# One core, FNet mixing with a gated FFN: the hidden transform's matrix sums made partly by adding DMAs, one input chunk brought back early into another buffer, two silus moved

## The chip, the cores and the metric

The kernel runs on one core of a Trainium2 chip. The time is device microseconds of one execution, smaller is better. The kernel before took 766.7 us (median of three runs, 765.25 to 767.39).

## The reference

```python
x = A_x                                   # 1 x 2048 x 448
xn = layernorm(x)
a, b = xn @ dft_hid_re.T, xn @ dft_hid_im.T     # 448 x 448 each
s = dft_seq_re @ a - dft_seq_im @ b             # 2048 x 2048 each
g = silu((gelu(xn @ w_gate) * (xn @ w_up)) @ w_down)   # 448 -> 1792 -> 448
out = x + s * g
```

All of it is float32. The kernel reaches that precision with float32r matmuls: a matrix is split into a high half (a copy rounded to float32r, made by ACT) and a low half (what is left, a subtraction on DVE), and a product is high·high + high·low + low·high.

## The kernel before

**Data.** The 2048 rows of x are 16 tiles of 128, in four chunks of four tiles. After the norm and the transposes, chunk c lies with its high and low half in the buffer `a_x[c]` (128 x 4096; `xt` in the profile).

**First stage, the FFN.** It runs from the start to about 397 us. The first two of the 14 feature blocks f are done plainly; the other twelve are done twice, for chunk pair p = 0 and p = 1, by a Strassen scheme: 24 calls of `strassen(f, p, ...)`, one after the other, a call taking PE 13.73 us in the steady state. In a call PE makes the products x1, x2, x3, x6, x4, then the second parts of x1, x6 and x4 (in this order, with the down products `po` of the group before between them). DVE adds the products up (L503, L511, L519, L539, L555 and others), ACT makes the gelu (L526, L558) and the high halves. Each product has a PSUM bank; the next call's x1 and x4 use the banks that this call's gelu (L526) and last addition (L555) read.

The lists `prep` and `dn` hold what else a call has to issue, at fixed places: `prep[0]` behind u (L503) and ahead of c21 (L511), `prep[1]` behind L519, `prep[2]` behind the gelu of x1. `prep` carries the weights of the next call: the low halves of the plain blocks and, on POOL, `sums_s` (five additions and subtractions, L337 to L343, of the raw weights); then ACT's high halves of these sums (`high`, L356, L357); then DVE's low halves (`low`, L360, L361) and SP's load of the weights for the call behind. Every third call adds two big DMAs (L957): the first terms of the sequence matrices' sums are copied from DRAM to DRAM, 896 KB each, and two calls later POOL issues two DMAs that add the second terms (L959; the queue `adds` is emptied inside `sums_s`, behind its first instruction).

**Matrices of the hidden transform.** The hidden transform uses the same scheme and needs sums of the blocks of its own matrices `et`. They are made in the calls of p = 1, appended to `prep` by `e_steps(f)`: in f = 5 to 9 five full-width subtractions, two full-width additions and a half-height subtraction of 448 columns (`e_sum`, L1054), two low halves of 896 columns (`es_low`, L1062) and, for the second set, high and low halves in f = 9 (L1067, L1068, L1071, L1075). The second set is stored to `eq` at f = 10 and loaded back at f = 13 (`eq_load`).

**Middle stage, the hidden transform.** Its order is the table `HID`, read word by word: `0.mm` are the 22 matmuls of row tile 0 (plain, tiles 0 to 7, chunks 0 and 1), `0.ev`, `0.sm`, `0.ca`, `0.lo` its way from PSUM (ACT), its sums (DVE, L1364 to L1367), high half (ACT, L1386) and low half (DVE, L1389). `P0` to `P3` are the paired tiles 8+kk and 12+kk. `s.3` and `s.all` are the last eight down products of the FFN (PE, L439, `po`), each followed by one DVE addition (L452); they use three PSUM banks in turn. Chunk 1 was written to DRAM (`sp`) in the first pass, since its buffer `a_x[1]` then held sums of chunk 2 and 3 until `P3`; `x.0` to `x.3` bring it back into `a_x[1]`, two DMAs each. Tile 4 (`4.mm`, L1266) is the first that reads it.

**Last stage, the sequence transform.** From about 477 us on, 8 output pairs j of 16 units: 14 units of seven products (`seven`, L1524 and L1527, 14 matmuls, some 2.18 us of PE each) and two plain ones (`py`, L1550). Each unit's matrix piece is loaded, summed (`sum_c`, L1434, L1435), and split by ACT (`high_c`, L1442) and DVE (`low_c`, L1446) three units ahead. All 14 transformed tiles (`TS`) stay in SBUF but four, in two pairs (`KX`), which are stored (`td`, POOL, L1391) and swapped in and out. At the end `gather` puts the seven products together on DVE, `g_` is the silu of the last two rows' gates, and L1645 to L1656 make and store the last two output tiles.

Instructions are issued in the order in which the code records them, on each engine's own queue.

Of the kernel before, what the change touches and what calls it, by code (L numbers as in the profile page):

```python
# [8 lines left out]
F32 = mybir.dt.float32  # L9
# [4 lines left out]
P = 128  # L14
# [28 lines left out]
KR = (8, 12, 9, 13, 10, 11, 4, 5, 6, 7)  # L43
KX = ((0, 1), (2, 3))
# [8 lines left out]
0.mm l.0 l.1 s.3 0.ev 0.sm 0.ca s.all 0.lo g.st 1.mm 1.ev 1.sm  # L53
# [3 lines left out]
P1.x4b P1.ae P1.se 3.mm P1.ce P1.lc 3.ev P1.le 3.sm  # L57
P2.x1 P2.m 3.ca P2.x2 P2.u P2.x3 P2.c21 P2.x4 P2.be 3.lo P2.x1b P2.ac P2.x6 P2.bc P2.sc
P2.x4b P2.ae
P3.x1 P3.m P2.ce P2.cc P3.x2 x.3 P3.u P3.x3 x.2 P3.c21 P2.le P3.x4 x.0 P3.be P2.lc P3.x1b P3.ac  # L60
P3.x6 x.1 P3.bc P3.sc P3.cc P3.x4b P3.ae c.l0
4.mm P3.ce P3.lc P3.le c.l1 c.l2 t.0 t.1 4.ev 4.sm 4.ca c.s0 c.s1
# [13 lines left out]
def fnet_geglu(ctx: ExitStack, tc: tile.TileContext, xw, ca, ct, cp, et, wss, wd, out):  # L76
# [495 lines left out]
    with tc.manual_schedule():  # L572
# [461 lines left out]
        eq = dram.tile([P, 6 * D], F32, name="eq")  # L1034
# [5 lines left out]
        def e_begin():  # L1040
            ew[0] = sb.tile([P, 4096], F32, name="ew", tag="u0")
            for b in range(2):
                nc.sync.dma_start(e_part(2 * b, 2), et[b].rearrange("p r d -> p (r d)"))

        def e_next():
# [6 lines left out]
        def e_sum(to, a, b, minus=True, n=P):  # L1052
            to, a, b = [e_part(i)[:n] for i in (to, a, b)]
            return lambda: (nc.vector.tensor_sub if minus else nc.vector.tensor_add)(to, a, b)  # L1054
# [698 lines left out]
```

## Time and profile before

| | us |
|---|---|
| median of three runs | 766.7 |
| the profiled execution | 767.89 |
| its span, first to last instruction | 766.1 |
| PE busy | 757.9 |
| DVE busy | 658.0 |
| ACT busy | 355.0 |
| POOL busy | 119.7 |

The granted PE clock is 1.00 over the whole span. Rows of a timeline read: start and length in us, engine, line, operation, output<-inputs, shapes, how many, and in brackets how long the engine was idle before and who ended that. In a table of waits a row reads: who waited <- for whom: us in total, times, longest. In the list of DMA issues the last number is the time from issue to landing. PE's matmuls overlap, so two rows' distance, not one row's length, is what a matmul costs.

### The profile page before, as it was taken

What the parts mean: (1) busy time and instruction counts of PE and PEld (TensorE: products, weight loads), DVE (VectorE), ACT (ScalarE), POOL (GpSimd) and SP (SyncE); (2) the same over time, 40 slices, a digit from 0 to 9 for tenths busy, and PEclk for the clock granted to TensorE, in tenths of its full rate; (3) what the DMA queues carried; (4) which work ended last, traced back from release to release, by engine and by line L of the source; (5) the groups of instructions that cost most, each with busy time, mean ns of one, the idle gap of its engine ahead of it and who ended that gap; (6) DMA issues with size and microseconds to landing.
All of it is one profiled execution on the core that took longest, in us unless ns stands there. A gap on an engine that the chain in (4) does not pass through costs nothing.

```text
span 766.1 us, 11581 instructions
## 1 busy us (share of the span) xinstructions
PE 757.9 (99%) x4033; PEld 681.8 (89%) x4033; DVE 658.0 (86%) x1121; ACT 355.0 (46%) x511; POOL 119.7 (16%) x160
## 2 busy tenths in 40 slices
PE   9999999999999999999999999999999999999997
PEld 8988888888888888888889988999999999999997
DVE  7987789899999889999876988788888797979796
ACT  6866443444434335343432546445445354444451
POOL 1002332412424224224200000000000000000000
PEclk9999999999999999999999999999999999999999
DMA  8077584949567784739544357779796969788793
GB/s 299 15 223 233 119 249 133 239 150 245 202 153 288 180 307 132 228 99 311 136 169 180 169 181 274 246 248 324 225 352 206 342 208 314 226 300 288 235 321 142
DMA packets 83643, 170.31 MB, mean 222 GB/s; under 512 B 8320, under 2 KB 63488, under 8 KB 81792
## 3 DMA queue, kind: packets, MB, share of 16 engines
q1 hardware_dynamic: 78256, 143.05, 53.8%
q0 software_dynamic: 5184, 26.41, 16.0%
q8 instruction: 31, 0.51, 0.3%
q14 instruction: 28, 0.23, 0.1%
q10 hardware_dynamic: 144, 0.11, 0.0%
HBM read 146.01 MB, written 52.63 MB: 259 GB/s over the span
## 4 chain that ended last, share of the span: by engine, by line
PE 86%; DVE 8%; DMA 2%; issue 2%; ACT 1%; SPq 0%; DVEq 0%
PE p L1524 21%; PE x L465 19%; PE po L439 15%; PE p L1527 10%; PE ab L1266 4%; PE py L1550 4%; PE hx L1305 4%; PE x L477 3%; PE gu L388 3%; PE gu L621 2%; PE pt L223 1%; DMA xt<-sp 1%; DVE tmp L562 1%; DVE ew L1054 1%; DVE gacc L452 1%
## 5 line engine op out<-in xcount | busy, mean ns | idle before, releaser
L439 PE MATMUL po<-wd,hs 128*128 128x448 f32 x672 | 146.1, 366 | 0.0
L439 PEld LDWEIGHTS po<-wd,hs 128*128 128x128 f32 x672 | 125.7, 188 | 12.5 <-DVE gacc L452 0.3
L465 PE MATMUL x<-xt,w 128*128 128x512 f32 x432 | 112.6, 391 | 0.5 <-DVE tmp L519 0.5
L465 PEld LDWEIGHTS x<-xt,w 128*128 128x128 f32 x432 | 80.8, 188 | 17.2 <-DVE tmp L519 1.4
L465 PE MATMUL x<-t,w 128*128 128x512 f32 x276 | 80.3, 390 | 0.7 <-DVE tmp L555 0.7
L1442 ACT ACTIVATE w<-raw 128x896 fp32r<-128x896 f32 (+1 forms) x58 | 52.7, 910 | 55.9 <-PE p L1524 21.2
L452 DVE TENSOR_TENSOR gacc<-gacc,po 128x448 f32<-128x448 f32 x96 | 58.7, 613 | 6.6 <-PE po L439 6.5
L542 ACT ACTIVATE hs<-tmp 128x512 fp32r<-128x512 f32 x24 | 15.2, 633 | 102.4 <-DVE tmp L540 102.4
L465 PEld LDWEIGHTS x<-t,w 128*128 128x128 f32 x276 | 51.7, 188 | 11.0 <-DVE tmp L555 1.1
L1576 POOL DMA_DIRECT2D cc<-xw x14 | 12.3, 879 | 280.8 <-DVE raw L1434 111.7
L1524 PE MATMUL p<-xt,xt 128*128 128x448 f32 x168 | 54.4, 374 | 0.0
L1524 PE MATMUL p<-ts_g,w 128*128 128x448 f32 x168 | 54.3, 374 | 0.0
L337 POOL TENSOR_TENSOR raw<-raw 128x256 f32<-128x256 f32 x23 | 20.0, 868 | 215.4 <-DMA raw<-wss 188.2
L1442 ACT ACTIVATE w<-f 128x896 fp32r<-128x896 f32 (+1 forms) x37 | 33.0, 892 | 40.5 <-PE p L1527 15.5
L1527 PE MATMUL p<-xt,xt 128*128 128x224 f32 x168 | 44.4, 264 | 0.0
L1527 PE MATMUL p<-ts_g,w 128*128 128x224 f32 x168 | 44.4, 264 | 0.0
L1446 DVE TENSOR_TENSOR w<-raw,w 128x896 fp32r<-128x896 f32 (+1 forms) x39 | 40.7, 1045 | 3.5 <-ACT w L1442 2.7
L1524 PE MATMUL p<-xt,w 128*128 128x448 f32 x112 | 36.4, 374 | 0.0
L1524 PE MATMUL p<-hs,w 128*128 128x448 f32 x112 | 36.0, 374 | 0.0
L1266 PE MATMUL ab<-w,xt 128*128 128x448 f32 x128 | 33.8, 369 | 1.5 <-DMA xt<-sp 1.5
L356 ACT ACTIVATE w<-raw 128x768 fp32r<-128x768 f32 x24 | 20.2, 843 | 31.8 <-POOL raw L343 31.6
L1524 PEld LDWEIGHTS p<-ts_g,w 128*128 128x128 f32 x168 | 31.5, 188 | 2.4
(304 smaller groups left out, 1865.0 us busy)
## 6 DMA issues: line engine op xcount, KB each, us to landing
sums<-ca SPq DMA_DIRECT2D x16, 896.0 KB, 8.7
sums<-ca POOLq DMA_DIRECT2D x16, 896.0 KB, 9.9
raw<-ct SPq DMA_DIRECT2D x69, 192.0 KB, 4.2
raw<-wss SPq DMA_DIRECT2D x24, 512.0 KB, 3.6
xt<-td SPq DMA_DIRECT2D x24, 448.0 KB, 5.5
ts_g<-td SPq DMA_DIRECT2D x24, 448.0 KB, 6.3
raw<-sums SPq DMA_DIRECT2D x69, 128.0 KB, 4.0
f<-ct SPq DMA_DIRECT2D x43, 192.0 KB, 3.6
```

Source lines behind the costliest of these rows:

```text
L388: nc.tensor.matmul(ps[:, cols], a, xt[:, k, cols], start=n == 0, stop=n == len(mm) - 1)
L439: nc.tensor.matmul(po[:, :D], hs[:, a, kk * P : (kk + 1) * P], wdn[:, b, i], start=n == 0, stop=n == 5,)
L452: nc.vector.tensor_add(ga, ga, po[:, :D])
L465: nc.tensor.matmul(ps, a[i], b[j], start=first and n == 0, stop=n == 2, skip_group_check=True)
L477: nc.tensor.matmul(ps, a[0], x_, start=False, stop=True, skip_group_check=True)
L1266: nc.tensor.matmul(ps[r], x_, e, start=start_, stop=stop_, skip_group_check=True)
L1305: nc.tensor.matmul(ps[i], a[:, sl], b, start=first and n == 0, stop=n == len(mm) - 1, skip_group_check=True,)
L1442: nc.scalar.activation(c_hl[m][0], raw_at(m)[:, :n], AF.Copy)
L1446: nc.vector.tensor_sub(l, raw_at(m)[:, : h.shape[-1]], h)
L1524: nc.tensor.matmul(ps[q][:, :D], h, v, start=u % UN == 0, stop=False, skip_group_check=True)
L1527: nc.tensor.matmul(ps[q][:, :HD], l, v[:, :HD], start=False, stop=u % UN == NS - 1, skip_group_check=True,)
L1550: nc.tensor.matmul(p[:, e], w, v[:, e], start=n == 0, stop=n == 11)
```

## The change

1. **Matrix sums.** Two sums of the hidden matrices are no longer made on DVE. `e_first()`, called at p = 1, f = 2, has SP copy two pieces of `et` from DRAM to DRAM (`e1`, 128 x 448 each) and appends three adding DMAs to `adds`, which POOL issues inside `sums_s` of that call. The first set's remaining sums stay in f = 5 and 6; its high half is recorded one place later (`prep[2]`), its low halves go to f = 7 and f = 9 behind L519; the second set's sums go from f = 8 to f = 11. The second set is stored raw, and its high and low halves (`eq_high`, `eq_low`) are made at the start of the middle stage: `q.h` behind `l.0`, `q.l` behind `s.3`.
2. **Chunk 1.** It comes back in one DMA (`x.1`) into chunk 0's buffer `a_x[0]`, recorded behind `3.mm`, the last tile of chunk 0. Tile 0's transform is loaded into `a_x[1]` (`t.0`) behind `P3.x6`, which moves ahead of `P3.x1b`. `4.mm` takes the usual order.
3. **Another tile is kept.** The pair (2, 3) that is swapped becomes (2, 8); tile 3 stays, in `a_h[1]`, and tile 8 is stored.
4. **Silus.** The two silus of the last pair stood ahead of the first copy of the last `gather`; now one stands a unit earlier and the other behind that copy; the loads of their inputs are one unit earlier.

```diff
-KR = (8, 12, 9, 13, 10, 11, 4, 5, 6, 7)
-KX = ((0, 1), (2, 3))
+KR = (12, 9, 13, 10, 3, 11, 4, 5, 6, 7)
+KX = ((0, 1), (2, 8))
 HID = """
-0.mm l.0 l.1 s.3 0.ev 0.sm 0.ca s.all 0.lo g.st 1.mm 1.ev 1.sm
+0.mm l.0 q.h l.1 s.3 q.l 0.ev 0.sm 0.ca s.all 0.lo g.st 1.mm 1.ev 1.sm
...
-P1.x4b P1.ae P1.se 3.mm P1.ce P1.lc 3.ev P1.le 3.sm
+P1.x4b P1.ae P1.se 3.mm x.1 P1.ce P1.lc 3.ev P1.le 3.sm
...
-P3.x1 P3.m P2.ce P2.cc P3.x2 x.3 P3.u P3.x3 x.2 P3.c21 P2.le P3.x4 x.0 P3.be P2.lc P3.x1b P3.ac
-P3.x6 x.1 P3.bc P3.sc P3.cc P3.x4b P3.ae c.l0
-4.mm P3.ce P3.lc P3.le c.l1 c.l2 t.0 t.1 4.ev 4.sm 4.ca c.s0 c.s1
+P3.x1 P3.m P2.ce P2.cc P3.x2 P3.u P3.x3 P3.c21 P2.le P3.x4 P3.be P3.x6 t.0 P2.lc P3.bc
+P3.x1b P3.ac P3.sc P3.cc P3.x4b P3.ae c.l0
+4.mm P3.ce P3.lc P3.le c.l1 c.l2 t.1 4.ev 4.sm 4.ca c.s0 c.s1
...
+        e1 = [dram.tile([P, D], F32, name=f"e1{i}") for i in range(2)]
+
+        def e_first():
+            for i in range(2):
+                nc.sync.dma_start(e1[i], et[3 * i, :, 1])
+            adds.append(lambda: nc.gpsimd.dma_start(e1[0], et[1, :, 1], accum_op=ALU.add))
             for r in (slice(0, 64), slice(64, P)):
-                nc.sync.dma_start(e_part(4)[r], et[2, :64, 1])
-            nc.sync.dma_start(e_part(7), et[2, :, 1])
...
+                adds.append(
+                    lambda r=r: nc.gpsimd.dma_start(e1[1][r], et[2, :64, 1], accum_op=ALU.add)
+                )
...
         def eq_high():
-            nc.scalar.activation(e_part(0, 2).bitcast(FR), e_part(7, 2), AF.Copy)
-            nc.scalar.activation(e_part(2, 2).bitcast(FR), e_part(5, 2), AF.Copy)
+            raw = a_r[:, 4 * D : 6 * D]
+            nc.scalar.activation(a_ws[:, 4480:][:, : 2 * D], eq_raw(), AF.Copy)
+            for i, k in enumerate((5, 4)):
+                nc.scalar.activation(eq_at(k), raw[:, i * D : (i + 1) * D], AF.Copy)
...
         def eq_low():
-            nc.vector.tensor_sub(e_part(7, 2).bitcast(FR), e_part(7, 2), e_part(0, 2))
-
-        def eq_stack():
-            h = e_part(2, 2)[64:]
-            nc.vector.tensor_sub(h.bitcast(FR), e_part(5, 2)[64:], h)
+            h = a_ws[:, 4480:][:, : 2 * D]
+            nc.vector.tensor_sub(a_ws[:, 4480 + 2 * D :][:, : 2 * D], eq_raw(), h)
+            raw = a_r[:, 4 * D : 6 * D]
+            for i, k in enumerate((5, 4)):
+                h = eq_at(k)[64:]
+                nc.vector.tensor_sub(h, raw[64:, i * D : (i + 1) * D], h.bitcast(F32))
...
-            if f == 5:
-                return [e_sum(4, 1, 3, False), e_sum(6, 0, 1), e_sum(5, 4, 0)]
-            if f == 6:
-                return [e_sum(7, 2, 5), es_high, es_low(0)]
-            if f == 7:
-                return [es_low(1), e_next]
-            if f == 8:
-                return [e_sum(5, 3, 4, False), then(e_sum(6, 2, 3), e_sum(7, 5, 2, n=64)), e_sum(8, 0, 7)]
-            if f == 9:
-                return [eq_high, eq_low, eq_stack]
-            return []
+            return {
+                5: [e_sum(6, 0, 1), e_sum(5, 4, 0)],
+                6: [e_sum(7, 2, 5), nop, es_high],
+                7: [nop, es_low(0)],
+                9: [nop, es_low(1), e_next],
+                11: [e_sum(6, 2, 3), e_sum(7, 5, 2, n=64), then(e_sum(8, 0, 7), eq_store)],
+            }.get(f, [])
...
                 dn[3] = then(send2, *t1_steps[7][:2])
+                e_first()
...
-            3: lambda: a_x[0],
+            3: lambda: a_h[1],
...
-            7: lambda: a_x[1],
+            7: lambda: a_x[0],
...
-        def load_1(k):
-
-            for i in range(2):
-                v, w = [u[:, 2048 * i + 512 * k :][:, :512] for u in (a_x[1].bitcast(F32), sp)]
-                nc.sync.dma_start(v, w)
+        def load_1():
+            nc.sync.dma_start(a_x[0].bitcast(F32), sp)
...
-        orders = {4: (3, 2, 0, 1), 7: (2, 0, 1, 3)}
+        orders = {7: (2, 0, 1, 3)}
...
-        GX_AT, GX_END = (NS, 0), NS - LAST - 3
+        GX_AT, GX_END = (NS, 0), NS - LAST - 4
...
                 prep_c(m + 3)
                 prep_c(m + 4)
-                for v, w in zip(g_, gx):
-                    nc.scalar.activation(v, w, AF.Silu)
 
                 c12_6, c11_2, c21_7, c12_5, c22_5, c12_3, c21_4 = gather(ps)
+                nc.scalar.activation(g_[0], gx[0], AF.Silu)
...
+                if end and u == NS - LAST - 1:
+                    nc.scalar.activation(g_[1], gx[1], AF.Silu)
```

Two places show how instructions move. Lines are those of the kernel that a listing belongs to; `[waits ...]` names the semaphores that an instruction waits for, DMAHW those of SP's DMAs, DMASW those of POOL's.

POOL in the call p = 1, f = 2, `sums_s` of the next weights, before:

```order
L337 TENSOR_TENSOR raw<-raw 128x2x128 [waits DMAHW4_49,DMAHW3_49,DVE_49]
L340 TENSOR_TENSOR raw<-raw 128x2x128
L341 TENSOR_TENSOR raw<-raw 128x128 [waits Pool_49]
L342 TENSOR_TENSOR raw<-raw 64x128
L343 TENSOR_TENSOR raw<-raw 128x256 [waits Pool_49]
```

and now (`e_813`, `e_814` are the two `e1`):

```order
L337 TENSOR_TENSOR raw<-raw 128x2x128 [waits DMAHW4_49,DMAHW3_49,DVE_49]
L1057 DMA e_813<-et 128x448 [waits DMAHW0_49,DMASW2_49]
L1060 DMA e_814<-et 64x448 [waits DMAHW1_49,DMASW3_49]
L1060 DMA e_814<-et 64x448 [waits DMASW4_49]
L340 TENSOR_TENSOR raw<-raw 128x2x128
L341 TENSOR_TENSOR raw<-raw 128x128 [waits Pool_49]
L342 TENSOR_TENSOR raw<-raw 64x128
L343 TENSOR_TENSOR raw<-raw 128x256 [waits Pool_49]
```

Between the first addition and the other four stand three DMA issues now, and the first two of them wait for SP's two copies of `et` into `e1`.

DVE at the start of the middle stage, the additions of the last down products (L452) and tile 0's sums (L1364 to L1367), before:

```order
L452 TENSOR_TENSOR gacc_2200<-gacc_2200,po_2_2_3447 128x448
L1364 TENSOR_TENSOR raw<-raw 128x224
L1365 TENSOR_TENSOR raw<-raw 128x224
L1366 TENSOR_TENSOR raw<-raw 128x224
L1367 TENSOR_TENSOR raw<-raw 128x224
L452 TENSOR_TENSOR gacc_2200<-gacc_2200,po_2_3_3462 128x448
```

and now:

```order
L452 TENSOR_TENSOR gacc_2207<-gacc_2207,po_2_2_3448 128x448
L1087 TENSOR_TENSOR w<-w 128x896
L1091 TENSOR_TENSOR w_3185<-raw,w_3185 64x448
L1091 TENSOR_TENSOR w<-raw,w 64x448
L1376 TENSOR_TENSOR raw<-raw 128x224
L1377 TENSOR_TENSOR raw<-raw 128x224
L1378 TENSOR_TENSOR raw<-raw 128x224
L1379 TENSOR_TENSOR raw<-raw 128x224
L452 TENSOR_TENSOR gacc_2207<-gacc_2207,po_2_3_3466 128x448
```

Three subtractions (`q.l`) stand between the third and the fourth addition of a down product, ahead of tile 0's sums.

More of the change, by code (lines that the diff above doesn't have):

```diff
@@ L1033, in fnet_geglu @@
         gv = gs.rearrange("p (k d) -> p k d", k=NK)
-        eq = dram.tile([P, 6 * D], F32, name="eq")
+        eq = dram.tile([P, 4 * D], F32, name="eq")
         ew, es, w2 = [None], [None], [None]
@@ L1329, in high_e @@
                     return
-                h, l = [rest(v) for v in ((new["tmp"], a_x[0]), (new["u1"], new["u0"]))[ke - 14]]
+                h, l = [rest(v) for v in ((new["tmp"], new["u1"]), (new["u0"], a_x[1]))[ke - 14]]
                 v = fs[ke][:, : 2 * D]
@@ L1412, in slot_at @@
                 lambda: (unit_at(2), unit_at(3)),
-                lambda: (unit_at(4), rest(a_x[1])),
+                lambda: (unit_at(4), rest(a_x[0])),
             )[m % 4]()
```

27 lines of the change are left out of this document (15 added, 12 removed).

## The prediction

> **What bounds the kernel now.** I read the page first, then PE's own waits, then PE's timeline call by call, and last the rows of the engines that PE waits for.
>
> ```profile
> PE 757.9 (99%) x4033; PEld 681.8 (89%) x4033; DVE 658.0 (86%) x1121; ACT 355.0 (46%) x511; POOL 119.7 (16%) x160
> ```
>
> PE is the bound, and the change leaves its matmuls as they are: the same number, another order. So only the few microseconds in which PE does not run can be won, and every new wait of PE is a loss. PE's waits in the middle of the kernel are three:
>
> ```profile
> PE ab L1266 <- DMA xt<-sp: 1.5, 1, 1.5
> ...
> PE x L465 <- DVE tmp L555: 0.7, 1, 0.7
> PE x L465 <- DVE tmp L519: 0.5, 1, 0.5
> ```
>
> A wait of PE costs a little more than its row, because the pipeline fills again. What they cost is read from the starts of the calls (x1 of f = 5, 6 and 11 in the second pass):
>
> ```profile
> 271.40 0.86 PE L465 MATMUL x<-xt,w 128*128 128x512 f32 x3
> ...
> 285.14 0.86 PE L465 MATMUL x<-xt,w 128*128 128x512 f32 x3
> ...
> 355.85 0.86 PE L465 MATMUL x<-xt,w 128*128 128x512 f32 x3
> ```
>
> f = 5 takes 285.14 - 271.40 = 13.74 us without a wait; six calls take 84.45, that is 2.05 us more than six times 13.73 or so (82.4). That is all there is in the first stage of this pass.
>
> **The change part by part.** The sum is made against the profiled execution, 767.89 us (its span 766.1), which is 1.2 us above the median 766.7; I apply it to the median.
>
> *A, the sums on DVE: -2.05.* DVE does its share of a call in order, so what the matrix sums add makes all behind them late. The first operation on x2 (L503) shows by how much:
>
> ```profile
> L1054 DVE TENSOR_TENSOR ew<-ew 128x448 f32<-128x448 f32 x7 | 5.4, 772 | 0.0
> ...
> 274.18 0.69 DVE L503 TENSOR_TENSOR tmp<-tmp,x 128x512 f32<-128x512 f32 x1 [1.51 <-PE x L465]
> ...
> 304.00 0.68 DVE L503 TENSOR_TENSOR tmp<-tmp,x 128x512 f32<-128x512 f32 x1
> ...
> 306.93 1.08 DVE L1062 TENSOR_TENSOR es<-ew,es 128x896 fp32r<-128x896 f32 x1
> ...
> 347.48 0.67 DVE L503 TENSOR_TENSOR tmp<-tmp,x 128x512 f32<-128x512 f32 x1
> ...
> 358.80 0.68 DVE L503 TENSOR_TENSOR tmp<-tmp,x 128x512 f32<-128x512 f32 x1
> ```
>
> At 274.18 DVE still waits for PE. Two calls on, PE's product is ready at 274.18 + 27.47 = 301.65, but DVE comes at 304.00, 2.35 late, and with L1062's 1.08 ahead of c21 it is 3.4 late at L519: PE stops for the 0.5. In the call from 347.48 to 358.80 DVE has no matrix work and needs 11.32 us, 2.4 less than PE. Up to that first stop the change takes out one full-width addition (0.77 by its group's row) and one low half (1.08), and moves the other low half behind L519, so DVE is some 2.9 less late there, far from a stop. Up to the second (L555, f = 9 to 10) f = 8's four operations and one of f = 9's two go as well. Three of these come back in f = 11: 3 x 0.77 = 2.3 in an odd call, which has another low half of its own, of 1.08 like L1062's; 11.32 + 1.08 + 2.3 = 14.7, one microsecond over PE's 13.73, well below the 3.4 at which PE stopped. I take all 2.05. The bounds are 1.0 (one stop stays) and 2.05.
>
> *B, chunk 1: -2.2, of which about 0.9 comes back, so -1.3.*
>
> ```profile
> 436.29 4.46 PE ab L1266 x22
> ...
> 456.40 2.37 PE L1266 MATMUL ab<-w,xt 128*128 128x448 f32 x10
> 460.30 1.70 PE L1266 MATMUL ab<-w,xt 128*128 128x448 f32 x6 [1.54 <-DMA xt<-sp]
> ...
> 463.09 0.37 PE L1266 MATMUL ab<-w,xt 128*128 128x448 f32 x1
> ```
>
> A tile needs 4.46; tile 4 took 463.09 - 456.40 = 6.69, so 2.23 are lost to the load. The new load waits for tile 3, whose 4.46 end at 440.75, and has 15 us until tile 4 at 456.40; it is 2 MB in one DMA, and a pair of 896 KB copies with a load behind it takes 9.1 us (in D). It is in time. But PE then reaches the last stage 2.23 earlier, and DVE does not:
>
> ```profile
> 463.25 0.39 DVE L1364 TENSOR_TENSOR f<-f 128x224 f32<-128x224 f32 x1 [0.63 <-ACT f L1374]
> ...
> 484.69 1.08 DVE L1446 TENSOR_TENSOR xt<-f,xt 128x896 fp32r<-128x896 f32 x1
> ...
> 485.50 0.38 PE L1524 MATMUL p<-w,xt 128*128 128x448 f32 x1
> 485.82 0.37 PE L1527 MATMUL p<-w,xt 128*128 128x224 f32 x1
> ```
>
> The first product of the fifth unit uses the high half at 485.50, and its second, with the low half, follows 0.32 later instead of the usual 0.21: DVE's 484.69 + 1.08 = 485.77 was only just in time. DVE is busy nearly throughout from tile 4's sums to there. It can move up by the 0.63 at its first row and by the short waits for ACT behind it, which I put at 0.7 together; 1.3 of 2.23. PE then waits some 0.9 at this unit. Bounds for B: 0 (DVE does not move up) and -2.23.
>
> *C, the silus: -0.35.*
>
> ```profile
> 751.62 1.04 ACT L1628 ACTIVATE raw<-ts_g 128x448 f32<-128x448 f32 x2 [0.23 <-DVE w L1446]
> ...
> 753.13 0.62 DVE L1559 TENSOR_TENSOR cc<-cc,p 128x448 f32<-128x448 f32 x1 [0.94 <-ACT cc L1557]
> ...
> 762.46 0.38 DVE L1650 TENSOR_TENSOR f<-raw,py 128x224 f32<-128x224 f32 x1
> ```
>
> From 753.13 on DVE runs to the end without a pause. The copy L1557 stood behind the two silus (751.62 + 1.04 = 752.66), and its product was done when the first of them began or shortly after: some 0.6 to be had. The last L1650 can come no earlier than PE's last matmul, around 762.0, so not all of that counts: 0.35. Bounds 0 and 0.45.
>
> *D, the adding DMAs in the call p = 1, f = 2: +3.8.* `sums_s` on POOL now holds three DMA issues, and the first two wait for SP's copies of `et`. Where do these stand on SP's queue? Right behind the pair of 896 KB copies, in the place of the load that followed them:
>
> ```profile
> 229.25 0.59 SPq L860 DMA_DIRECT2D tmp<-xw  x1
> ...
> tmp<-xw SPq DMA_DIRECT2D x1, 256.0 KB, 9.1
> ...
> 217.68 1.65 POOL L959 DMA_DIRECT2D sums<-ca  x2
> ...
> 221.44 0.73 POOL L343 TENSOR_TENSOR raw<-raw 128x256 f32<-128x256 f32 x1
> ...
> 232.00 0.87 POOL L337 TENSOR_TENSOR raw<-raw 128x256 f32<-128x256 f32 x1 [9.82 <-DMA raw<-wss]
> ...
> 234.93 1.21 POOL L343 TENSOR_TENSOR raw<-raw 128x256 f32<-128x256 f32 x1
> ...
> 236.17 0.85 ACT L356 ACTIVATE w<-raw 128x768 fp32r<-128x768 f32 x1 [1.87 <-POOL raw L343]
> ...
> 237.97 0.95 DVE L360 TENSOR_TENSOR w<-raw,w 128x768 fp32r<-128x768 f32 x1
> ...
> 245.28 0.60 ACT L497 ACTIVATE tmp<-x 128x512 f32<-128x512 f32 x1
> ...
> 248.71 1.52 PE L465 MATMUL x<-xt,w 128*128 128x512 f32 x6
> ```
>
> That load of 256 KB landed 9.1 us after its issue, at 238.35. A copy of 224 KB in its place lands about then, the second at about 239.2 (0.6 later issued, and as many bytes again). POOL is through with L337 at 232.9 and now stands until 238.35. A DMA issue takes it 1.65 / 2 = 0.83. The second adding DMA starts at 239.2, the third at 240.0. In the call with two of them the second began at 218.5 and L343 ended at 222.17, 3.7 later; here it ends at 240.0 + 3.7 = 243.7 instead of 236.14, 7.55 late. Behind it: ACT's high half L356 and, queued after it on ACT, the gelu of x1; DVE's L360, which reads L356 and had 0.95 in hand (237.97 - 237.02), so it is 6.6 late, with all of DVE behind it, closely packed to L555 and the next sum; ACT's copy L497 of the next call's x1 stands behind these and ends at 245.88 + 6.6 = 252.5. PE needs that copy for the second part of x1, at 248.71. It waits 252.5 - 248.7 = 3.8 us (on the way it waits for the gelu's bank and for L555's; these waits are inside the 3.8). By the next calls the lateness is eaten up by DVE's spare time. No stop of PE comes as long as POOL is less than 0.95 + (248.71 - 245.88) = 3.8 late. Bounds: 0, if the copies land by 232.9; and, by the longest landing of a smaller DMA behind such a pair,
>
> ```profile
> sp<-xt SPq DMA_DIRECT2D x2, 512.0 KB, 11.2
> ```
>
> 229.85 + 11.2 = 241.05 for the second copy, 1.85 later: +5.7.
>
> [...]
>
> *E, the second set's halves in the middle stage: +1.15.*
>
> ```profile
> 401.84 9.73 PE po L439 x48
> ...
> 394.11 1.16 DVE L1107 TENSOR_TENSOR w<-raw,w 64x448 fp32r<-64x448 f32 x2
> ...
> 406.06 0.39 DVE L1364 TENSOR_TENSOR raw<-raw 128x224 f32<-128x224 f32 x1
> ...
> 407.40 1.18 DVE L452 TENSOR_TENSOR gacc<-gacc,po 128x448 f32<-128x448 f32 x2
> ```
>
> Eight down products take 9.73, 1.22 each. With three banks the seventh, at 401.68 + 7.3 = 409.0, needs the fourth's addition, the first of the two at 407.40, over at 408.0: 1.0 to spare. Now `q.l` goes in at 406.06: a subtraction of 896 columns (1.08 as L1062, 1.0 of it apart from the next) and two like L1107's pair (1.1): 2.1 us. The addition ends at 410.1, and the seventh product waits 1.15. ACT's three copies of `q.h` are done before that. The rest of the stage only shifts. Bounds 0 and +1.3.
>
> Hidden, and taken as nothing: the store of tile 8's transform and the swap of (2, 8), as many bytes at other times, the buffer needed again some 15 us later; the store of `eq` and its load, two instead of four DMAs; the order of P3.
>
> The sum: -2.05 - 1.3 - 0.35 + 3.8 + 1.15 = **+1.25**. The profiled execution would come to 769.1, the median to **768.0**.
>
> **The rivals.** *The copies are no obstacle* (D = 0): they would have to land in 3.6 us, as the weights' loads do over the whole kernel:
>
> ```profile
> raw<-wss SPq DMA_DIRECT2D x24, 512.0 KB, 3.6
> ```
>
> Then POOL is less than 3.8 late, and -2.05 - 1.3 - 0.35 + 1.15 gives -2.55: 764.2. Against it stands the 9.1 in this very place; for it, that a copy writes to DRAM and may be served beside the others. *Slower*: POOL stands longer. The mechanism is the same wait, at its upper price 5.7, because DRAM-to-DRAM rows behind 1.8 MB already under way take longer than the load did; +3.15, or 769.9. It passes the 0.3% bound when the second copy lands after about 240.2, 11 us after the first one's issue. *The change does not do what it says*: DVE keeps its stops, because POOL's work stretches its operations in f = 7 as before and f = 11 is now the fullest; A = 0 with the rest as forecast gives +3.3, 770.0. Against it is DVE's 2.4 us of spare time in a call without matrix work.
>
> **How the numbers follow.** A measurement of this kernel tells about 0.3%, 2.3 us, from no change. The forecast (D between 2.4 and 4.8, net -0.2 to +2.3) has 0.50; the copies no obstacle 0.27; POOL standing longer 0.13; DVE's stops staying 0.10. The second is faster by 0.33% and, with E or the giving back in B smaller, by up to 4 us: of its 0.27 I count 0.22 as faster. Faster 0.24 (0.02 for a forecast with small D), same 0.50, slower 0.26 (the last two, and 0.03 from the forecast's upper end). The forecast's own range is 766.5 to 769.0; the one to hold 8 in 10 goes from 763.8, a little below the first rival, to 770.5, above the slow ones.
>
> **What would show it.** D: in the call f = 2 of the second pass POOL has a row between L337 and L340 that waits for a DMA of `e1` for some 5 us, the wait of ACT's L356 for POOL grows from 1.87 to over 7, and PE has one to three waits of together 3.8 between the x1 of f = 3 and the second part of it. A: no wait of PE for L519 or L555 in f = 5 to 11, and L503 of f = 7 less than 1 us behind PE. B: tile 4 in 4.5 us, and a wait of PE near 1 us in the fifth unit of the last stage. C: L1557 directly behind its product. E: a wait of about 1.15 of a down product for L452. Wrong is the forecast if POOL's added issues wait for nothing, or if PE does not stop though POOL is 7 us late.

## The result, and the profile after

The changed kernel takes **774.1 us** (median of six runs, 773.3 to 775.7); the kernel before took 767.5 beside it (765.3 to 769.0). The ratio is 1.009, with a 95% interval of 1.007 to 1.011: slower by 0.9%, where 768.0 and no measurable difference had been forecast. The profiled execution took 774.05, its span 772.3, against 767.89 and 766.1 before: 6.2 us.

The work per engine is what it was (from the page of the changed kernel):

```profile
PE 759.8 (98%) x4033; PEld 683.5 (89%) x4033; DVE 654.2 (85%) x1120; ACT 355.4 (46%) x512; POOL 120.1 (16%) x163
```

PE has the same 4033 matmuls and is 1.9 us longer busy with them (most of that is a slower clock, told below); DVE is 3.8 us less busy. The rest of the difference is in PE's waits. The view of waits of the changed kernel, PE alone (total, times, longest):

```profile
PE x L477 <- ACT xt L880: 2.7, 1, 2.7
PE po L439 <- DVE gacc L452: 1.4, 2, 1.2
PE x L465 <- ACT tmp L526: 1.2, 1, 1.2
PE p L1537 <- DVE xt L1458: 0.9, 1, 0.9
PE x L477 <- DVE xt L884: 0.8, 1, 0.8
```

The three old ones (L1266 for `sp`, L465 for L555 and for L519) are gone, as forecast. Three new ones lie in one call, f = 3 of the second pass (L526, L880, L884); of the two waits for L452 the one of 1.25 is the middle stage's, the other (0.15) lies in f = 12; L1458 is the last stage's fifth unit.

Where the 6.2 us are is read from the starts of the same PE work in both timelines, here of the changed kernel (x1 of f = 4 and 11, tile 0, tile 1, the first product `py`),

```profile
265.48 0.86 PE L465 MATMUL x<-xt,w 128*128 128x512 f32 x3
...
361.62 0.86 PE L465 MATMUL x<-xt,w 128*128 128x512 f32 x3
...
403.26 0.36 PE L1278 MATMUL ab<-w,xt 128*128 128x448 f32 x1
...
418.95 0.37 PE L1278 MATMUL ab<-w,xt 128*128 128x448 f32 x1
...
513.70 0.37 PE L1560 MATMUL py<-ts_tmp,w 128*128 128x448 f32 x1
```

and set against the kernel before (its x1 of f = 11 stands in the prediction):

```profile
257.67 0.86 PE L465 MATMUL x<-xt,w 128*128 128x512 f32 x3
...
397.22 0.36 PE L1266 MATMUL ab<-w,xt 128*128 128x448 f32 x1
...
411.40 0.36 PE L1266 MATMUL ab<-w,xt 128*128 128x448 f32 x1
...
507.66 0.38 PE L1550 MATMUL py<-ts_tmp,w 128*128 128x448 f32 x1
```

| up to | before | after | later by | so the step | forecast |
|---|---|---|---|---|---|
| x1 of f = 4 | 257.67 | 265.48 | 7.81 (0.13 of it from the start of the pass) | D: +7.7 | +3.8 |
| x1 of f = 11 | 355.85 | 361.62 | 5.77 | A: -2.04 | -2.05 |
| tile 0 | 397.22 | 403.26 | 6.04 | +0.27, in f = 12, behind f = 11's sums | 0 |
| tile 1 | 411.40 | 418.95 | 7.55 | E: +1.51 | +1.15 |
| first `py` | 507.66 | 513.70 | 6.04 | B: -1.51 | -1.3 |
| the end | 766.1 | 772.3 | 6.2 | C: +0.2 | -0.35 |

The miss in the profiled executions is 6.2 - 1.25 = 4.95 us. One term carries most of it: D, 3.9 us too small. C was 0.5 short of its forecast, E 0.4 too small, and the 0.27 was not forecast; B was 0.2 better, and 0.1 lies ahead of the pass.

### The profile page after: what moved, and what is told of

The parts are those of the page before. It is cut to its first block, busy times and chain, and to the rows that moved or that the text cites. A ratio compares the mean times of both kernels' runs of the same rounds, so it can differ in the third digit from the quotient of the medians.

```text
span 772.3 us, 11563 instructions
## 1 busy us (share of the span) xinstructions
PE 759.8 (98%) x4033; PEld 683.5 (89%) x4033; DVE 654.2 (85%) x1120; ACT 355.4 (46%) x512; POOL 120.1 (16%) x163
## 4 chain that ended last, share of the span: by engine, by line
PE 83%; DVE 10%; DMA 3%; issue 2%; POOL 1%; ACT 1%; SPq 0%; DVEq 0%; POOLq 0%
PE p L1534 19%; PE x L465 18%; PE po L439 13%; PE p L1537 9%; PE ab L1278 5%; PE py L1560 4%; PE hx L1317 4%; PE x L477 3%; PE gu L388 3%; PE gu L621 2%; DMA e<-et 1%; DMA raw<-cp 1%; PE pt L223 1%; DVE gacc L452 1%; DMA out<-cc 1%
## 5 line engine op out<-in xcount | busy, mean ns | idle before, releaser
L465 PE MATMUL x<-xt,w 128*128 128x512 f32 x432 | 113.3, 393 | 1.2 <-ACT tmp L526 1.2
L465 PEld LDWEIGHTS x<-xt,w 128*128 128x128 f32 x432 | 81.9, 190 | 17.8 <-ACT tmp L526 1.6
L465 PE MATMUL x<-t,w 128*128 128x512 f32 x276 | 80.5, 391 | 0.0
L452 DVE TENSOR_TENSOR gacc<-gacc,po 128x448 f32<-128x448 f32 x96 | 58.6, 614 | 6.2 <-PE po L439 6.0
L465 PEld LDWEIGHTS x<-t,w 128*128 128x128 f32 x276 | 51.7, 188 | 10.3 <-DVE tmp L544 0.4
L337 POOL TENSOR_TENSOR raw<-raw 128x256 f32<-128x256 f32 x23 | 18.8, 817 | 214.4 <-DMA raw<-wss 164.7
L1537 PE MATMUL p<-xt,xt 128*128 128x224 f32 x168 | 44.4, 264 | 0.0
L1537 PE MATMUL p<-ts_g,w 128*128 128x224 f32 x168 | 44.4, 264 | 0.0
L1458 DVE TENSOR_TENSOR w<-raw,w 128x896 fp32r<-128x896 f32 (+1 forms) x39 | 40.6, 1045 | 1.8 <-ACT w L1454 1.1
L356 ACT ACTIVATE w<-raw 128x768 fp32r<-128x768 f32 x24 | 20.3, 844 | 37.1 <-POOL raw L343 36.9
L477 PE MATMUL x<-xt,w 128*128 128x512 f32 x98 | 31.1, 397 | 3.5 <-ACT xt L880 2.7
```

The source lines that it names most:

```text
L452: nc.vector.tensor_add(ga, ga, po[:, :D])
L465: nc.tensor.matmul(ps, a[i], b[j], start=first and n == 0, stop=n == 2, skip_group_check=True)
L477: nc.tensor.matmul(ps, a[0], x_, start=False, stop=True, skip_group_check=True)
L1458: nc.vector.tensor_sub(l, raw_at(m)[:, : h.shape[-1]], h)
L1537: nc.tensor.matmul(ps[q][:, :HD], l, v[:, :HD], start=False, stop=u % UN == NS - 1, skip_group_check=True,)
```

## The experiments

### What happens in the call f = 2 and 3

First the trace of the changed kernel. POOL, in `sums_s` of the call f = 2, then ACT and DVE behind it, then PE in the call f = 3 (four timelines of the same execution; ahead of them the row of the two copies `e1` in its list of DMA issues):

```profile
e<-et SPq DMA_DIRECT2D x2, 224.0 KB, 9.1
...
231.84 0.80 POOL L337 TENSOR_TENSOR raw<-raw 128x256 f32<-128x256 f32 x1 [9.89 <-DMA raw<-wss]
238.82 0.81 POOL L1057 DMA_DIRECT2D e<-et  x1 [6.18 <-DMA e<-et]
239.36 1.93 POOL L1060 DMA_DIRECT2D e<-et  x2
...
242.96 0.73 POOL L343 TENSOR_TENSOR raw<-raw 128x256 f32<-128x256 f32 x1
...
243.72 0.84 ACT L356 ACTIVATE w<-raw 128x768 fp32r<-128x768 f32 x1 [9.65 <-POOL raw L343]
...
251.41 0.63 ACT L880 ACTIVATE xt<-tmp 128x512 fp32r<-128x512 f32 x1 [0.62 <-DVE tmp L875]
251.94 0.58 ACT L497 ACTIVATE tmp<-x 128x512 f32<-128x512 f32 x1
...
244.60 0.96 DVE L360 TENSOR_TENSOR w<-raw,w 128x768 fp32r<-128x768 f32 x1 [7.01 <-ACT w L356]
...
252.43 0.94 DVE L884 TENSOR_TENSOR xt<-tmp,xt 128x512 fp32r<-128x512 f32 x1
...
245.41 0.96 PE L465 MATMUL x<-xt,w 128*128 128x512 f32 x3 [1.19 <-ACT tmp L526]
...
252.09 0.49 PE L477 MATMUL x<-xt,w 128*128 128x512 f32 x1 [2.66 <-ACT xt L880]
253.42 0.50 PE L477 MATMUL x<-xt,w 128*128 128x512 f32 x1 [0.84 <-DVE xt L884]
```

Up to ACT's copy nearly all is as forecast: the copies landed 9.1 us after their issue, POOL stood until 238.82 (forecast 238.35), L343 ended at 243.69 (forecast 243.7), L360 was 6.6 late (forecast 6.6), and L497 ended at 252.52 (forecast 252.5). But L497 is not what PE waited for. Ahead of it in PE's order stands x3's second part (L477, two matmuls of which one reads a high half that ACT writes at L880, the other a low half that DVE writes at L884; both belong to the steps in `dn[3]` of the call f = 2). In the kernel before that low half was the tight one:

```profile
244.66 0.63 ACT L880 ACTIVATE xt<-tmp 128x512 fp32r<-128x512 f32 x1 [0.50 <-DVE tmp L875]
...
245.69 1.23 DVE L884 TENSOR_TENSOR xt<-tmp,xt 128x512 fp32r<-128x512 f32 x1
...
247.12 0.62 PE L477 MATMUL x<-xt,w 128*128 128x512 f32 x2
```

The low half was over at 246.92. PE came to the pair at 247.12, and to its second matmul, which reads the low half, at about 247.35 (247.12 + 0.23): 0.4 us in hand, and not the 2.8 that L497 had. The high half, over at 245.29, had 1.8. Now the second matmul starts at 253.42, 6.07 later, 5.9 of it behind the start of the pass. The remaining 1.7 of D come behind that, with no wait of PE: the view of windows shows it, with PE's busy time and its granted clock (the column ahead of the DMA share).

```profile
253.00:254.00 1.00, 0.58 (x3) 1.00 0.92 387
254.00:255.00 1.00, 1.00 (x5) 0.67 0.35 143
255.00:256.00 1.00, 1.00 (x4) 0.50 0.24 100
256.00:257.00 1.00, 1.00 (x4) 0.50 0.04 14
257.00:258.00 1.00, 1.00 (x4) 0.62 0.00 0
258.00:259.00 1.00, 1.00 (x7) 1.00 0.06 16
```

From 254.3 to 257.8, some 3.4 us, PE ran at half clock: half of 3.4 is the 1.7. **The theory** is thus: POOL's wait for the copies, through DVE's lateness, stops PE for 5.9 us, and PE's idleness then lowers the clock. **The rivals**: the DMA traffic itself, or the load of `tmp` that now stands behind two more DMAs; too many adding DMAs in one place; another part of the change; and, for the clock, chance.

### The copies one call earlier

```diff
-        def e_first():
+        def e_copy():
             for i in range(2):
                 nc.sync.dma_start(e1[i], et[3 * i, :, 1])
+        def e_first(adds=adds):
             adds.append(...)
...
+                elif f == 13:          # p = 0
+                    e_copy()
```

> The changed kernel, with SP's two copies of `et` into `e1` issued one call earlier (p = 0, f = 13), ahead of the pair of 896 KB copies. POOL's three adding DMAs stay where they are, in `sums_s` of p = 1, f = 2. Theory (POOL stands for the two copies, the weights' halves behind it come late, and PE stops at the third product of the call f = 3 and then runs at half clock): the copies are long done when POOL comes, POOL's three issues cost 3 x 0.81 us and no more, L343 ends near 236.2 + 0.8, no stop in f = 3 and no granted clock below 1 there; x1 of f = 4 starts near 257.7 + 0.1, and the whole comes 7.7 us lower, at 774.1 - 7.7 = 766.4. Rival 1 (three adding DMAs in one place are too much by themselves, copies or not): L343 stays later than 239.9 and at least 3 us of the 7.7 stay, 769.5 or more. Rival 2 (the load of `tmp` from `xw`, which the copies push back on SP's queue, is what comes late): that is mended here as well, so this run does not tell it from the theory; the next one does.

Measured: 766.2 (ten runs, 765.7 to 766.6), ratio 0.9993 [0.9983, 1.0002]. POOL does not wait for the copies:

```profile
232.75 0.81 POOL L1059 DMA_DIRECT2D e<-et  x1
233.30 1.93 POOL L1062 DMA_DIRECT2D e<-et  x2
...
237.34 0.74 POOL L343 TENSOR_TENSOR raw<-raw 128x256 f32<-128x256 f32 x1
```

Of the three stops one of 0.2 is left (L884), the clock stays at 1.00 from 254 to 259, and x1 of f = 4 starts at 258.31. The loss of 7.7 falls to 0.5 (258.31 - 257.67, less 0.11 from the start of the pass). The expectation was a little too kind here: three issues that wait for nothing make L343 end at 238.08, 1.9 later than in the kernel before and not 0.8, and this is already enough for the small stop. Rival 1 falls.

### The adding DMAs behind the five sums

```diff
+        while adds_2:                 # behind L343 in sums_s
+            adds_2.pop(0)()
...
-                e_first()
+                e_copy()
+                e_first(adds_2)
```

> The changed kernel, with the two copies in their place on SP, but the three adding DMAs issued by POOL behind the five sums of `sums_s` in the same call, so that POOL stands there as before, with nothing of the weights' halves behind it. Theory (the lateness goes from POOL's wait through L343 to ACT's L356 and DVE's L360): L343 ends near 235.0 to 236.2, before POOL's wait, no stop in f = 3, 774.1 - 7.7 = 766.4. Rival 1 (the traffic of copies and adding DMAs, or the load of `tmp` from `xw` that now stands behind two more DMAs on SP's queue, makes the call late): nothing of that changes here, so the time stays within 1.5 us of 774.1. Rival 2 (POOL's later stand makes POOL's next work late, that of f = 3): some 2 to 4 us of the 7.7 stay, 768.5 to 770.5.

Measured: 765.9 (765.7 to 767.1), ratio 0.9982 [0.9972, 0.9992]. POOL still waits for the copies, but with L343 behind it already:

```profile
234.89 1.20 POOL L343 TENSOR_TENSOR raw<-raw 128x256 f32<-128x256 f32 x1
239.07 0.82 POOL L1061 DMA_DIRECT2D e<-et  x1 [2.98 <-DMA e<-et]
239.62 1.93 POOL L1064 DMA_DIRECT2D e<-et  x2
```

All DMAs, their traffic and their place on SP's queue are those of the changed kernel, and the whole 7.7 is gone: L343 ends at 236.09 (236.14 in the kernel before) and x1 of f = 4 starts at 257.71 (257.67). So it is not the traffic and not the load of `tmp`; it is what stands behind the waiting instruction on POOL.

### Only the five DMAs, in the kernel before

```diff
+        e1 = [dram.tile([P, D], F32, name=f"e1{i}") for i in range(2)]
+        def e_first():                # as in the change
...
                 dn[3] = then(send2, *t1_steps[7][:2])
+                e_first()
```

> The kernel before, with nothing of the change but the two copies into `e1` and the three adding DMAs, at the places that they have in the changed kernel; what they make is not read (the sums are still made on DVE), so this is added work alone. Theory (these five DMAs are the whole loss of the first stage): the wait of ACT's L356 for POOL is above 9 us, PE stops in f = 3 and loses 7.7 us there, 767.5 + 7.7 = 775.2; a little may be taken back at the two stops of f = 6 and f = 9 to 10 which the kernel before keeps, no more than 0.3. Rival (the loss comes from another part, the buffers u0 and a_x[0] or the order of the sums): no more than 1 us is lost, 767 to 768.5.

Measured: 776.4 (773.5 to 780.0), ratio 1.0127 [1.0093, 1.0160]. ACT's L356 waits 10.5 us for POOL, and PE stops in f = 3 as in the changed kernel. So these DMAs alone make the loss. It is 1.2 us more than expected, with a wide spread. In the profiled execution the copies took 10.0 us to land in place of 9.1, and PE's first stop was 2.0 in place of 1.2. The clock fell earlier there and for two such stretches, from 252.1 to 259.0 (6.8 us):

```profile
252.00:253.00 1.00, 0.15 (x1) 0.57 0.98 308
253.00:254.00 1.00, 0.64 (x1) 0.50 0.90 351
```

### The copies ahead of the big pair

```diff
+            if (p, f) == (1, 2):
+                e_copy()
             sum_step(n)               # issues the pair of 896 KB copies
```

> The changed kernel, with SP's two copies into `e1` in the same call as before, but issued right ahead of the pair of 896 KB copies (L957) on SP's queue and not behind it. The adding DMAs stay in their place. Theory (a copy's landing 9 us after its issue is the pair ahead of it on the same queue, so its place among SP's issues decides, not the call): the copies land in some 3 us, by 232 to 233, POOL does not wait for them, no stop in f = 3, and the time is that of the run with the copies one call earlier, 766.2 (765.7 to 766.8). Rival (the pair is under way on the same DMA engines and slows whatever runs beside it, ahead or behind): the copies land 6 us or more after their issue, POOL waits at least 2 us, and 1 to 4 us of the 7.7 stay, 767.5 to 770.5.

Measured: 768.2 (767.1 to 770.5), ratio 1.0007 [0.9996, 1.0018], 1.1 us above the copies one call earlier when each is taken by its ratio to the kernel before (0.0014 of 767), and 2.0 by the starts of x1 of f = 4 in the two profiles (260.27 and 258.31). The rival is right, but for POOL's wait, which was 1.91 and not quite the 2 that it asked for. The DMA issues of 227 to 230 us, with the median time from issue to landing last, and POOL's timeline:

```profile
sums<-ca SPq DMA_DIRECT2D x2, 896.0 KB, 9.0
raw<-wd SPq DMA_DIRECT2D x1, 448.0 KB, 6.1
e<-et SPq DMA_DIRECT2D x2, 224.0 KB, 6.2
...
234.62 0.81 POOL L1059 DMA_DIRECT2D e<-et  x1 [1.91 <-DMA e<-et]
```

Ahead of the pair the copies still took 6.2 us, with 448 KB of weights ahead of them and the pair beside; one call earlier, 4.1. POOL's stand of 1.9 made L343 end at 239.86, 3.7 later than in the kernel before, and PE stopped 1.17 for L880 and 0.84 for L884. The prediction had said that PE stops only when POOL is over 3.8 late. The clock stayed at 1.00 behind this pair of stops.

### PE kept at work during its stops

```diff
+        x6 = x_tile(6)
+        if q and (f, p) == (3, 1):    # between the two parts of x3
+            for _ in range(4):
+                three(x6, w["a11"], b11, True)
...
```

> The changed kernel as it is, with twelve matmuls more that nobody reads (x1's first product four times over, into x6's bank, which x6 then starts anew), put on PE in the call p = 1, f = 3 between the two parts of x3, where PE stood 2.66 us for ACT's L880. They fill the stand and take about 12 x 0.23 = 2.8 us; the wait itself stays. Theory (of the 7.7 us lost by the start of f = 4 some 6.0 are waits, and 1.7 come from the half clock that was granted for 3.4 us from 254.3 on, because PE had little to do in the time before): with PE at work the granted clock stays at 1.00 throughout, the twelve cost nothing but the 0.1 or 0.2 by which they outlast the wait, and the whole takes 774.1 - 1.7 = 772.4 (772.2 to 772.8). Rival (the low clock is not tied to PE's own idleness, but came by chance or from the DMAs beside it): the clock falls to 0.50 as well, and the time stays at 774.1 or grows by the twelve, to 774.3.

Measured: 772.8 (772.1 to 773.6), ratio 1.0066 [1.0052, 1.0080]. The time is near the theory's, but the clock did fall in the profiled execution, only earlier. There the copies landed later (10.6 us), so that PE stood 2.68 us at x1, ahead of the filled place; the clock was 0.50 from 248.4 to 251.9. The mean granted clock, which is on record for each run, parts the four runs in the same way: 0.997 in those of 773.4 and 773.6, 1.00 in those of 772.1 and 772.2. So both stops were filled, and the unchanged kernel was run beside it:

```diff
+        hold = q and (f, p) == (3, 1)
+        if hold:                      # ahead of x1
+            x2, x6 = x_tile(2), x_tile(6)
+            for _ in range(3):
+                three(x2, w["a22"], b11, True)
...
+        if hold:                      # between the two parts of x3
+            for _ in range(4):
+                three(x6, w["a22"], b11, True)
...
```

> The changed kernel once more, unchanged, as the measure for the three that run beside it on the same chip: 774.1 (773.3 to 775.7), and in the profile the half clock near 254 or elsewhere in the call f = 3 of the second pass.

> The changed kernel as it is, with matmuls that nobody reads at both stands of PE in the call p = 1, f = 3, since with one stand filled the clock fell behind the other: nine ahead of x1 (2.1 us, into x2's bank, which DVE has long read) and twelve between the two parts of x3 (2.8 us, into x6's bank). All waits of DVE, ACT and POOL stay. Theory (the half clock follows from PE's own idleness and costs 1.7 us on top of the 6.0 of waits): PE is never idle for more than 1 us there, the granted clock stays at 1.00 in every microsecond of the call, and the time is 774.1 - 1.7 = 772.4, with no run above 773. Rival 1 (the low clock comes by chance or from the DMAs beside it): it falls to 0.50 in this call again, 774.1 or more. Rival 2 (the filling itself outlasts the waits and costs as much as the clock did): clock 1.00, and 773.5 or more.

Measured: 775.4 (773.3 to 776.1), ratio 1.0100 [1.0086, 1.0114] for the unchanged one, with 3.4 us of half clock from 254.0 on in its profile; 772.05 (771.9 to 774.1), 1.0069 [1.0056, 1.0081] with both stops filled, which is 2.4 us less by the ratios (0.0031 of 767). With the twenty-one matmuls in place PE's wait for L884 is still 0.85, the clock is 1.00 throughout,

```profile
254.00:255.00 1.00, 1.00 (x6) 1.00 0.46 181
255.00:256.00 1.00, 1.00 (x6) 1.00 0.26 108
```

and the down products of f = 3 start at 256.26, against 257.76 in the unchanged kernel beside it: 1.5 us won by matmuls whose products nobody reads. It is not one profile alone: the mean granted clock of the changed kernel was 0.996 or 0.998 in each of its eleven runs, and 1.00 in each of the five with both stops filled. A mean alone would not prove it, since the clock can also fall behind PE's last matmul, where it costs nothing (0.50 from 761 on in the profile of the run that only takes the sums out, below), and the kernel before has runs at 0.998 too. With the profiles it does: PE's idle time is what lowers the clock here, with the DMAs and the waits of the other engines as they were. The 2.4 of the ratios are more than the 1.7 that one stretch of half clock costs, but the two intervals together leave room for 1.7. One of the five runs, 774.1, is above the 773 that the theory allowed; its clock was 1.00, so the half clock is not the reason, and which it is stays open. The Trainium skill, "TensorE: Matmul & The Clock Gate", section "Part 1: The HAM clock gate", describes this: a free-running window of 3.4 us, half clock after an idle one, full clock after a busy one. The stretches of 3.4 and 6.8 us agree with it. An idle window is not to be taken as one without any work: here 2.66 and 0.84 us of idle time with a matmul between them were enough.

### The second set's halves behind tile 0's low half

```diff
-0.mm l.0 q.h l.1 s.3 q.l 0.ev 0.sm 0.ca s.all 0.lo g.st 1.mm 1.ev 1.sm
+0.mm l.0 q.h l.1 s.3 0.ev 0.sm 0.ca s.all 0.lo q.l g.st 1.mm 1.ev 1.sm
```

(with the copies one call earlier)

> The changed kernel with the copies one call earlier, as in the first of these runs, and in the middle stage's table with `q.l` (a subtraction of 896 columns and two half-height ones on DVE) behind `0.lo` in place of ahead of `0.ev`. Theory (the three DVE operations stood ahead of the fourth down product's addition, and PE lost 1.50 us there): the wait of `po` for L452 goes, tile 1 starts 1.5 us earlier, 766.4 - 1.5 = 764.9. Rival 1 (the time comes back: what was lost there was also lost by DVE, and PE arrives at the last stage's fifth unit before its operand and waits longer, 0.9 us now): 766.4 - 1.5 + up to 1.5, that is 765.5 to 766.4, with a wait of the product L1537 for L1458 of over 1.5 us. Rival 2 (tile 0's `0.sm` and low half take their place and the wait only moves to tile 1 or 2): 766.4.

Measured: 765.3 (764.0 to 765.6), ratio 0.9976 [0.9965, 0.9986]. In the unchanged kernel PE's row was

```profile
416.42 2.70 PE L439 MATMUL po<-wd,hs 128*128 128x448 f32 x12 [1.25 <-DVE gacc L452]
```

and this wait is now 0.2. The spans, 764.0 and 762.3, differ by 1.7, the medians by 0.9, where 1.5 was expected; by the ratios it is 1.3 (0.0017 of 767). The wait at the last stage's fifth unit is 0.5 in both, so nothing comes back there. It was run once more:

> The changed kernel with both mendings (copies one call earlier, `q.l` behind `0.lo`) once more, beside the unchanged one and with more rounds, as the version that should beat both kernels: ratio to the kernel before 0.998, that is some 1.5 us below the kernel before and 8.8 below the changed one. Rival (the first ratio of 0.9976 was the chip's drift): 1.000.

Measured: 764.5 (763.9 to 765.7), ratio 0.9967 [0.9955, 0.9980]. This version beats both kernels: 0.3% under the kernel before, 1.3% under the change.

### The sums spread or only taken out

```diff
-                5: [e_sum(6, 0, 1), e_sum(5, 4, 0)],
-                6: [e_sum(7, 2, 5), nop, es_high],
-                7: [nop, es_low(0)],
-                9: [nop, es_low(1), e_next],
-                11: [e_sum(6, 2, 3), e_sum(7, 5, 2, n=64), then(e_sum(8, 0, 7), eq_store)],
+                5: [nop, e_sum(6, 0, 1), e_sum(5, 4, 0)],
+                6: [e_sum(7, 2, 5), es_high, es_low(0)],
+                7: [es_low(1), e_next],
+                8: [nop, then(e_sum(6, 2, 3), e_sum(7, 5, 2, n=64)), then(e_sum(8, 0, 7), eq_store)],
```

> The version with both mendings, with DVE's share of the matrix sums put back into the calls where the kernel before has them (f = 5: two subtractions, 6: one and a low half, 7: a low half, 8: the rest and the store), while the two additions that the adding DMAs make and the halves of the second set stay away from there. So the part `spread` is undone and the part `by DMA and later` is kept. Theory (what removed PE's two stops of f = 6 and f = 9 to 10 is the taking out, 0.77 us per addition, and not the spreading: DVE was 3.4 us late at the first stop, which was 0.5 long, so 0.77 less is enough; the second was 0.7 long, and 0.77 and the halves of f = 9 are away): no stop of PE for L519 or L555, time as of the version with both mendings within 0.3 us. Rival (the spreading counts): both stops or one of them come back, 1.0 to 2.0 us more than that version.

Measured: 764.8 (764.2 to 765.7), ratio 0.9971 [0.9960, 0.9981], as the version with both mendings. PE has no wait for L519 or L555. What A won is won by the two additions that DMAs make and the halves that moved out of f = 9, taken together; neither was tried alone. The spreading over later calls added nothing to it. With the sums out of f = 11 PE takes 41.35 from x1 of f = 11 to tile 0, as in the kernel before (41.37); in the changed kernel it takes 41.64, the 0.27 of the table. It is not lost every time: with the copies one call earlier it is 41.36, with the same sums in f = 11.

### The silus

```diff
-        GX_AT, GX_END = (NS, 0), NS - LAST - 4
+        GX_AT, GX_END = (NS, 0), NS - LAST - 3
...
+                for v, w in zip(g_, gx):
+                    nc.scalar.activation(v, w, AF.Silu)
                 c12_6, c11_2, c21_7, c12_5, c22_5, c12_3, c21_4 = gather(ps)
-                nc.scalar.activation(g_[0], gx[0], AF.Silu)
...
-                if end and u == NS - LAST - 1:
-                    nc.scalar.activation(g_[1], gx[1], AF.Silu)
```

(on the version with both mendings; the second run leaves `GX_END` as in the change)

> The best so far (copies one call earlier, `q.l` behind `0.lo`; 765.3) with the move of the silus undone: both silus stand ahead of the sums' copy L557 of the last stage's end again (L1571 here), and the loads of their inputs one unit later, as in the kernel before. Theory (the move does win what was forecast, where the loads of the last units are not late): from PE's last matmul to the end it took 4.15 us in the kernel before and 3.76 with the silus moved, so 765.3 + 0.4 = 765.7. Rival 1 (the move wins nothing; what is seen in the tail is DMA's doing): 765.3, within 0.1. Rival 2 (the loads that stand earlier cost time at the end): 765.0 or less.

> As the run before it, with the silus put back but the loads of their inputs left where the change puts them, one unit earlier. Theory (only the silus' place on ACT counts): 765.7, as the run before. Rival (the place of the loads counts, the silus' not): 765.3, as with both moved.

Measured: 765.7 (765.0 to 766.9), ratio 0.9975 [0.9964, 0.9985] with all undone; 764.9 (764.1 to 765.5), 0.9963 [0.9950, 0.9975] with the loads left. With both moved it was 0.9976 and 0.9967 in its two sessions. The whole time does not settle it: the intervals overlap. The tail does, in the profiled executions. The first sum behind the copy L1557 (L1571 here) with the silus put back, and the same copy with them moved:

```profile
750.45 0.62 DVE L1573 TENSOR_TENSOR cc<-cc,p 128x448 f32<-128x448 f32 x1 [1.22 <-ACT cc L1571]
```

```profile
748.29 0.55 ACT L1571 ACTIVATE cc<-p 128x448 f32<-128x448 f32 x1 [0.47 <-PE p L1541]
```

Put back, DVE waits 1.22 for a copy that stands behind the silus (0.70 in the run that leaves the loads one unit earlier); moved, the copy itself waits for its product. From PE's last matmul to the end it is 4.4 us with all undone, 4.2 with the silus alone put back, 3.7 with both moved. In the changed kernel, however, it was 4.3, against 4.15 before. There a load of the last units came late, and everything on DVE and ACT behind it:

```profile
754.06 0.29 DVE L1446 TENSOR_TENSOR f<-f 128x128 f32<-128x128 f32 x1 [2.29 <-DMA f<-sums]
...
758.12 0.53 ACT L1567 ACTIVATE cc<-p 128x448 f32<-128x448 f32 x1
```

The same wait is 0.5 long in the first run of the version with both mendings. The DMA engines have no pause in the ten microseconds ahead of it in either (250 to 420 GB/s), so there is little in which a late load could catch up. Why it came late in that execution was not tried.

## Why the prediction was wrong, step by step

**D** is the step that failed. Its mechanism stood: POOL between L337 and L340 waits for the copies `e1` behind the big pair, and the weights' halves behind it are late. So did its times, to a tenth, for L343, L360 and L497. What failed is the sentence "PE needs that copy for the second part of x1, at 248.71. It waits 252.5 - 248.7 = 3.8 us". It took L497 for the first thing that PE needs of the late engines, and it is not the first. Everything behind L360 on DVE was late by nearly the same amount, and what PE needs of it before L497 is the pair of L880 and L884, the latter with 0.4 us in hand and not 2.8. With it the wait would have been priced at 6.6 - 0.4 = 6.2; 5.9 was measured. The same choice made the threshold too kind, 3.8 where 0.95 + 0.4 = 1.4 is right: at 1.9 late PE stopped for 0.2, and at 3.7 twice. The second part of the miss, 1.7, is a cost that no wait shows: the half clock behind the idle time, which the sum did not have at all. Neither was in the bounds, which ended at 5.7; the rival "POOL stands longer" had the sign, but a mechanism that did not occur. The copies took 9.1 us, as in the forecast.

**A** came as forecast, -2.04 for -2.05: L503 of f = 7 waits for PE again, 1.45, where DVE had been 2.35 late. That the sums of f = 11 cost nothing did not come true: 0.27 is lost again in the call behind, where PE waits 0.15 for L452. The runs add that the spreading had no part in the gain.

**B** came as forecast, -1.51 for -1.3: tile 4 takes 4.5 us in place of 6.69, and so did the price at the fifth unit: the wait of L1537 for L1458 is 0.9.

**C** was not won in the changed kernel (+0.2). The step's reason is borne out, in single profiled executions, where the loads are in time (3.7 against 4.15 and 4.4); left out was that the tail also depends on the last loads, in a stage whose DMA engines have no pause up to its end.

**E** was right in place and mechanism and too small: 1.51 for 1.15. The row says 1.25; the rest is the pipeline that drains and fills again, as the prediction itself had said of waits (the twelve matmuls behind the wait take 2.70, and 2.60 where they follow others).

What the forecast named as its own disproof (POOL's issues wait for nothing, or PE does not stop) did not occur. The sum of the measured terms is 7.7 - 2.0 + 0.3 + 1.5 - 1.5 + 0.2 = 6.2, with D at 5.9 + 1.7.

## What to carry to other kernels

When an engine that works in order comes late, list everything behind the late instruction that the bounding engine reads, in the order in which that engine reads it, and price the wait at the first with little in hand, not at the one that is easiest to see. A wait on a helper engine need not cost anything by itself (POOL's 2.98 behind the sums cost nothing): put it behind the work that others need (766 in place of 774 here, with the same transfers), or issue what it waits for so early that a big transfer on the same queue is neither ahead of it nor beside it. And a stop of PE can have a second price, the clock behind it: here it came with every stop of 2.56 to 2.68 us, and cost 1.7 us or twice that.

## What the runs showed of the hardware

The half clock was not expected. It followed on 1.19, 2.66 and 0.84 us of idle time within 10 us, on 2.02 and the first 1.9 of 2.64, and on one idle time of 2.68; it did not follow on 1.17 with 0.84 behind it, nor on a single 1.25 or 1.54. In the 3.4 us just ahead of each of the four falls in the profiles PE was idle for 1.9 to 2.3 us in all; 1.17 and 0.84 make 2.0 as well, so the sum alone does not decide, and what does is open. The half clock lasted 3.4 us, or 6.8 where PE was still waiting in its first 3.4, and so it also widens the spread between runs: with the five DMAs alone the runs of 773.5, 776.3, 776.4 and 780.0 had a mean granted clock of 0.998, 0.995, 0.995 and 0.993.

A small copy of 224 KB took 9.0 to 10.6 us behind the pair of 896 KB (six profiles), 6.2 ahead of it on the same queue, and 4.1 a call earlier. To be issued first is not to be served alone.

In one profiled execution, that of the copies ahead of the pair, the same matmuls of the middle stage took 2% longer than in the run with the copies a call earlier, with no wait and at a clock shown as 1.00: from the first pair's products to the third's 25.21 us, against 24.72.

```profile
418.32 1.19 PE L1321 MATMUL hx<-w,xt 128*128 128x448 f32 x5
...
443.53 1.20 PE L1321 MATMUL hx<-w,xt 128*128 128x448 f32 x5
```

```profile
415.96 1.18 PE L1321 MATMUL hx<-w,xt 128*128 128x448 f32 x5
...
440.68 1.18 PE L1321 MATMUL hx<-w,xt 128*128 128x448 f32 x5
```

It came to 1.3 us by the first `py` of that execution (509.36 and 505.81, less the 2.2 by which tile 0 was late). Its cause is open.
